# Lightweight convolution and a three-way maxout FFN on one core: weights loaded in two column pieces, an undivided band, block 1's conv copied by ScalarE, x6's load released by a memset

## The chip, the core and the metric

The kernel runs on one core of a Trainium2 chip. The metric is the device time of the whole program in microseconds (us). TensorE (PE) multiplies matrices, and its weight loads are listed apart as PEld; VectorE is DVE, ScalarE is ACT, GpSimd is POOL. SyncE (SP) does no arithmetic here: it issues nearly all the DMAs, from one queue and in program order. Matmul results go to PSUM, from where ScalarE and VectorE copy them on; all other tiles lie in SBUF.

## The reference, cut to what matters

```python
# x: (8, 4160, 192); weight: (8 heads, 7 taps); w1, w2, w3: (192, 768); w_out: (768, 192)
w = softmax(weight, axis=-1)                    # per head
x_pad = 6 zero rows ahead of each sequence
y[b, s, h, :] = sum_k w[h, k] * x_pad[b, s + k, h, :]      # causal conv, 24 channels a head
y = y.reshape(33280, 192)
h = maximum(maximum(y @ w1, y @ w2), y @ w3)
out = h @ w_out                                  # float32, (33280, 192)
```

Every token is convolved over its own and the six tokens before it, with one set of seven weights for each head. Then come three projections to 768 columns, their elementwise maximum, and one projection back.

## The kernel before, in words

**Tiling.** The 33280 tokens are cut into 65 blocks of 512. The 768 hidden columns are cut into 6 groups of 128, called columns 0 to 5 here. The maximum is taken as w3's product plus max(relu(y(w1-w3)), y(w2-w3)). So the kernel builds `wd`, the differences w1-w3 (n=0) and w2-w3 (n=1) for the first 128 input channels and a third slice (n=2) that holds both differences for the last 64 channels (`make_wd`, L318). The share of w3 itself goes through a product of w3 and w_out (`transpose_w3`, `make_m`). For each column `top` (L503) does a relu on ScalarE (L508), which reads the PSUM tile `lp` or `lw`, and a maximum on VectorE (L509), which reads `lq` or `lw` and writes `h`. Then `h` is multiplied by `wo` (L585 and L616).

**The band.** The conv is a matmul against a banded matrix `band`, [128 rows, 8 heads, 134 columns]. Its windows of 38 columns are equal in each quarter of 32 rows. 38 small matmuls (L291) make one window in two PSUM tiles, columns 0 to 27 and 28 to 37. ScalarE copies the first tile and VectorE the second (L299) into all four quarters, heads 5 to 7 first and then heads 0 to 4; block 0's conv begins with the part that needs only heads 5 to 7.

**Dense blocks.** Blocks 0 to 3 are convolved by `conv_dense` (L384). x is loaded into `xin` (float32) and cast to two float16 tiles `xz` by `cast_dense` (L207), where the slots of 32 channels can be given. Two halves of matmuls (n=0: channel slots 0 to 3, n=1: slots 4 and 5) go to two PSUM tiles; `order` says which half is first, and `copies[n]` copies half n to `yd`. The first columns of blocks 0 and 1 are multiplied by `l1_dense`, as full products ("F", from half 0 of `yd`) and half-height products ("H", from half 1 and the slice n=2 of `wd`). Blocks 0 and 1 take turns, two columns at a time.

**Later blocks** (4 and on) are loaded with a layout of 39 rows (`load_x`), their gap rows zeroed first (`zero_x`), cast by GpSimd (`cast_x`, L199), convolved (L375), copied (L415), transposed by a DMA (L429) and multiplied (L521). Their buffers are shared; blocks 4, 5 and 6 have buffers of their own, block 7 takes block 0's. Blocks 5 and 6 are convolved together.

**The order of the work** is written out by hand: each engine runs its instructions as they stand in the program, and semaphores make them wait. SP's DMAs use eight completion semaphores in turn, so a DMA is not issued before the eighth one ahead of it (counting ScalarE's one load) has landed.

**The weights' loads** go to a float32 tile `wall` with the parts `ws` and `w3s`. `load_wa(f)` (L227) loads columns f of the first 128 channels of w3, w1 and w2 in three transfers; `load_wb(f)` (L231) loads the last 64 channels of w1 and w2 in two; L244 loads the last 64 channels of w3 whole. Before, columns 0 to 255, 256 to 511 and 512 to 767 of `load_wa` are three pieces, with `load_wb` of the rest between the second and the third: L243 to L245 and L303 to L305. `copy_w3` (L322, profile line L324) doubles w3's last 64 channels to the other half of the partitions, which the slice n=2 of `wd` needs.

**The start from L695 on** is the part that the diff rearranges. ScalarE and VectorE share the copies of block 1's conv (L702). Then stand ScalarE's second `copy_w3`, GpSimd's subtractions for columns 2 to 5 (L704 to L707), GpSimd's casts of w3 and w_out, and the first products and relus. `zero_x(6)` (L715, profile line L140) is ScalarE's zeroing of block 6's gap rows, and L716 issues the loads of blocks 4, 5 and 6. Block 2's conv stands at L733, block 7's load at L741.

Of the kernel before, what the change touches and what calls it, by code (L numbers as in the profile page):

```python
# [15 lines left out]
P = 128  # L16
KW = 7
PAD = KW - 1
NHEAD = 8
# [5 lines left out]
WIN = 32 + PAD  # L25
# [3 lines left out]
def kernel(  # L29
# [12 lines left out]
    nc = tc.nc  # L42
# [3 lines left out]
    H, KWs = weight.shape  # L46
    assert H == NHEAD and KWs == KW and D == GRP * NHEAD
    DFF = moe_w1.shape[1]
# [9 lines left out]
    for b in range(B):  # L58
        s = nfull * NBLK
        while s < SEQ:  # L60
            n = min(SEQ - s, NBLK - off)
# [24 lines left out]
    NDENSE = 4  # L86
    chunks_of = [conv_chunks(blk) for blk in blocks[:NDENSE]]
    NQ = len(chunks_of[0])
    TOK = 32
# [29 lines left out]
    xin, xbuf, XBUF, loaded = {}, [], 7, set()  # L119

    def get_x(t):

        if not 0 <= t < NB or t in xin:
            return
        if t < XBUF:
            xbuf.append(const.tile([P, NR, D], FP32, name=f"xf_{t}"))
        xf = xbuf[t % XBUF if t < NDENSE + XBUF else NDENSE + (t - NDENSE - XBUF) % 3]
        assert all(v[0] is not xf for v in xin.values())
        xin[t] = [xf, 0, ()]

    def zero_x(t, q0=0, q1=NR, eng=None):
# [4 lines left out]
        if eng is not None:  # L136
# [4 lines left out]
                       in_=bass.AP(tensor=zero.tensor, offset=zero.offset,  # L141
                                   ap=[list(zero.ap[0]), [0, q1 - q0], [1, D]]))

    def load_x(t, eng=nc.sync):
        if not 0 <= t < NB:
            return
        loaded.add(t)
        get_x(t)
        xf = xin[t][0]
        if t < NDENSE:  # L150
            todo = [(0, c[3], c[1] * SEQ + c[2], i) for i, c in enumerate(chunks_of[t])]
        else:
            todo = [(HALF * (i // NR) + (0 if s else LAP), KR if s else TOK,
                     b * SEQ + s - (LAP if s else 0), i % NR) for i, (b, s) in enumerate(rows_of(t))]
        parts = []
        i, n = 0, len(todo)
        row = [c[2] for c in todo]
        while i < n:
            k = i
            while k + 1 < n and todo[k + 1][:2] == todo[i][:2] and row[k + 1] - row[k] == row[i + 1] - row[i]:  # L160
                k += 1
            step = row[i + 1] - row[i] if k > i else 0
            p0, rlen, _, q0 = todo[i]
            q1 = todo[k][3] + 1
            src = bass.AP(tensor=x.tensor, offset=row[i] * D,
                          ap=[[D, rlen], [step * D, q1 - q0], [1, D]])
            eng.dma_start(out=xf[p0:p0 + rlen, q0:q1, :], in_=src)  # L167
            if parts and parts[-1][0] == rlen:
                parts[-1] = (rlen, parts[-1][1], q1)
            else:  # L170
                parts.append((rlen, q0, q1))
            i = k + 1
        xin[t] = [xf, todo[0][0], parts]
# [12 lines left out]
    def cast_x(t):  # L186
        if not 0 <= t < NB:
            return
        xf, p0, _ = xin.pop(t)
        t0, u, nu = place(t)  # L190
        if u == 0:
            pool = x16q if nu >= 4 else x16p
            x16 = pool.tile([P, NHEAD * 4 * 2 * GRP * (5 if nu >= 4 else nu)], FP16, tag="x16", name=f"x16_{t0}")
            x16s[t0] = x16[:, 0:NHEAD * 4 * 2 * GRP * nu].rearrange("p (h j u r c) -> p h j u r c", h=NHEAD, j=4, u=nu, r=2)
        if p0:
            nc.gpsimd.memset(xf[0:p0, 0, :], 0.0)
        K = HALF + KR
        for r in range(2):
            nc.gpsimd.tensor_copy(out=x16s[t0][0:K, :, :, u, r, :].rearrange("p h j c -> p j h c"),  # L199
                                  in_=xf[0:K, 4 * r:4 * r + 4, :].rearrange("p j (h c) -> p j h c", c=GRP))  # L200

    NC, NSLOT, CYC = D // HALF, D // 32, 96
# [1 line left out]
    xz = {t: [const.tile([P, NQ, D], FP16, name=f"xz_{t}_{v}") for v in range(2)] for t in range(2)}  # L204
    xz[2], xz[3] = xz[0], xz[1]

    def cast_dense(t, copies, slots_=range(CYC // 32), keep=False):  # L207
        xf, _, parts = xin[t] if keep else xin.pop(t)
        for v, copy in enumerate(copies):
            if copy is None:  # L210
                continue
            for s in slots_:
                cut = GRP * (32 * s // GRP + 1)
                a, b = (32 * s, cut) if v == 0 else (cut, 32 * s + 32)
                for (rl, q0, q1) in parts:
                    copy(  # L216
                        out=xz[t][v][0:rl, q0:q1, :].rearrange("p q (k c) -> p q k c", c=CYC)[:, :, :, a:b],
                        in_=xf[0:rl, q0:q1, :].rearrange("p q (k c) -> p q k c", c=CYC)[:, :, :, a:b])
# [6 lines left out]
    PW = 2 * P  # L225

    def load_wa(f):  # L227
        for st, n, wsrc in ((w3s, 0, moe_w3), (ws, 0, moe_w1), (ws, 1, moe_w2)):
            nc.sync.dma_start(out=st[:, n, f], in_=wsrc[0:P, f])  # L229
# [51 lines left out]
    nc.vector.reciprocal(out=wrec[:], in_=wrec[:])  # L281
    zero_x(4)
    nc.vector.tensor_scalar_mul(out=line[0:NHEAD, 31:31 + KW], in0=wexp[:, 0:KW], scalar1=wrec[:])
    cast_dense(0, (nc.vector.tensor_copy, nc.gpsimd.tensor_copy), (1, 2), keep=True)
    CUT = 28
    bands_ = []
    for lo, hi, copy in ((0, CUT, nc.scalar.copy), (CUT, WIN, nc.vector.tensor_copy)):
# [5 lines left out]
                             rhs=ident16[:, 0:4 * NHEAD], start=True, stop=True)  # L293
        bands_.append((lo, hi, copy, bps))
    keep_warm((NBLK, NBLK, P), psp, "p")
    for h0, h1 in ((5, NHEAD), (0, 5)):
        for lo, hi, copy, bps in bands_:
            for a in range(4):
                copy(out=band[32 * a:32 * a + 32, h0:h1, 32 * a + lo:32 * a + hi],  # L299
                     in_=bps[:, 0:hi - lo, h0:h1].rearrange("p c h -> p h c"))  # L300
        if h0:
            cast_dense(0, (nc.vector.tensor_copy, nc.gpsimd.tensor_copy), (0,))
    load_wa(slice(PW, 2 * PW))  # L303
    load_wb(slice(PW, DFF))
    load_wa(slice(2 * PW, DFF))  # L305
    nc.sync.dma_start(out=wos[:], in_=moe_w_out.rearrange("(j p) c -> p j c", p=P))
    load_x(2)
    load_x(3)

# [8 lines left out]
    def make_wd(n, j0, j1, eng=nc.vector):  # L318
        f = slice(P * j0, P * j1)
        eng.tensor_sub(out=wd[:, n, f], in0=ws[:, n, f], in1=w3s[:, n // 2, f])  # L320
# [63 lines left out]
    def conv_dense(t, copies, pools=((None, None),) * 2, order=(0, 1)):  # L384


        yd = dense[t] = ydp.tile([P, NC, NBLK], FP16, tag="yd", name=f"yd_{t}")
        for n in order:
            slots_ = ((0, 1, 2, 3), (4, 5, 4, 5))[n]
            pool, tag = pools[n]  # L390
            ps = (pool or psw).tile([P, NBLK], FP32, tag=tag or "w", name=f"D{n}_{t}")
            for (q, b, row_lo, rlen, lo, hi, cc) in chunks_of[t]:
                for v in range(2):
                    for g, s in enumerate(slots_):
                        h = (32 * s + 31 * v) // GRP
                        nc.tensor.matmul(  # L396
                            ps[32 * g:32 * g + 32, lo:hi],
                            lhsT=xz[t][v][0:rlen, q, 32 * s:32 * s + 32],
                            rhs=band[0:rlen, h, cc:cc + hi - lo],
                            start=(v == 0), stop=(v == 1), tile_position=(0, 32 * g))  # L400
            copies[n](out=yd[:, 2 * n, :], in_=ps[:])
# [129 lines left out]
    def l1_dense(tiles, parts="FH"):  # L531

        meet()
        for n, part in enumerate(parts):
            for t, j, pools in tiles:
                for i, (pool, tag) in enumerate(pools):
                    if (t, j, i) not in open_ps:
                        open_ps[t, j, i] = pool.tile([P, NBLK], FP32, tag=tag, name=f"l{tag}{i}_{t}_{j}")
                        begun.discard((t, j, i))
                    if part == "F":  # L540
                        a, b = wd[:, i, P * j:P * (j + 1)], dense[t][:, 0, :]
                    else:
                        a, b = w_of(i, NC - 1, j), y_all(t, i, NC - 1)
                    nc.tensor.matmul(open_ps[t, j, i][:], lhsT=a, rhs=b,  # L544
                                     start=(t, j, i) not in begun, stop=(t, j, i) in begun)
                    begun.add((t, j, i))

    def tops(*tiles):
        for t, j in tiles:
            top(t, j, (open_ps[t, j, 0], open_ps[t, j, 1]))  # L550
# [141 lines left out]
    WPWQ = ((psw, "w"), (psp, "p"), (psw, "w"), (psq, "q"))  # L692
    ACT, DVE = nc.scalar.copy, nc.vector.tensor_copy
    GP = nc.gpsimd.tensor_copy
    conv_dense(0, (ACT, ACT), order=(1, 0))  # L695
    cast_dense(1, (DVE, GP), (1, 2, 0))
    zero_x(5, eng=nc.gpsimd)
    make_wd(0, 0, 2)
    make_wd(1, 0, 2)
    copy_w3(ACT, 0, 2)  # L700
    make_wd(2, 0, 2)
    conv_dense(1, (DVE, ACT), order=(1, 0))  # L702
    copy_w3(ACT, 2, 6)
    for n in range(NC):  # L704
        make_wd(n, 2, 4, nc.gpsimd)
    for n in range(NC):
        make_wd(n, 4, 6, nc.gpsimd)  # L707
    cast_w3(0, 6)
    GP(out=wo[:], in_=wos[:])
    l1_dense([(0, 0, PQ), (0, 1, PQ)], "F")  # L710
    l1_dense([(0, 0, PQ), (0, 1, PQ)], "H")
    tops((0, 0), (0, 1))
    l1_dense([(1, 0, WW), (1, 1, WW)], "HF")
    tops((1, 0), (1, 1))
    zero_x(6)  # L715
    for t in range(NDENSE, XBUF):  # L716
        load_x(t)
    l1_dense([(0, 2, PQ), (0, 3, PQ)], "FH")
    tops((0, 2), (0, 3))
# [11 lines left out]
    first_hidden(0)  # L731
    first_hidden(1)
    conv_dense(2, (ACT, DVE), (WW[0], PQ[1]))  # L733
    cast_x(4)
    cross(2, ACT, DVE)
    make_m(0)
# [114 lines left out]
```

## Time and profile before

| what | us |
|---|---|
| median of 3 runs | 453.19 (453.03 to 454.11) |
| the profiled execution | 454.16 |
| its span | 452.4 |
| PE busy in the span | 445.5 |
| VectorE, ScalarE, GpSimd busy | 354.6, 320.2, 207.6 |
| first product of layer 1 on PE begins | 8.94 |
| mean granted TensorE clock | 1.00 |

The profile lists each engine's instructions with start and length, what each engine waited for, the DMA queues with their packets, and a "chain": the work that ended last, followed back from the last instruction, each step to what released it. A time with two decimals is one from the span's start. The DMA share is the mean busy share of the 16 DMA engines. Queue q1 holds SP's transfers, q8 and q14 carry instructions.

### The profile page before, as it was taken

To read this page: it belongs to the slowest core of one execution; us is meant where nothing else is said; L and a number is where in the kernel's file an instruction comes from. 1 tells how busy PE (TensorE), PEld (TensorE's weight loads), DVE (VectorE), ACT (ScalarE), POOL (GpSimd) and SP (SyncE) were. 2 spreads that over 40 slices of the span, in tenths; PEclk is the share of its full clock that TensorE was granted. 3 is DMA by queue.
4 is the path that set the end of the run, shared out by engine and by line. 5 is a ranking of instruction groups with operands and counts; after the bars stand their busy time and mean duration, and the time that the engine had idled before them with its cause. 6 is when DMAs were issued, how large, how long until landed. Compare 5 with 4: busy or idle time off the path is not lost.

```text
span 452.4 us, 18264 instructions
## 1 busy us (share of the span) xinstructions
PE 445.5 (98%) x7576; PEld 409.8 (91%) x7576; DVE 354.6 (78%) x607; ACT 320.2 (71%) x601; POOL 207.6 (46%) x239
## 2 busy tenths in 40 slices
PE   7999999999999999999999999999999999999997
PEld 4469999999999989999999999999999999999996
DVE  6668787878878787787887787887887887887775
ACT  6967767767777677676676776777776776776664
POOL 5864836556463533724824635525533644224000
PEclk9999999999999999999999999999999999999999
DMA  7968987696885659649649748657649668152123
GB/s 197 239 181 167 203 186 197 155 217 171 170 220 147 165 137 205 162 121 199 167 127 198 178 110 191 191 114 193 178 112 197 172 157 143 54 136 75 58 71 106
DMA packets 128163, 72.01 MB, mean 159 GB/s; under 512 B 52305, under 2 KB 127888, under 8 KB 128080
## 3 DMA queue, kind: packets, MB, share of 16 engines
q1 hardware_dynamic: 127919, 70.75, 65.9%
q8 instruction: 59, 0.97, 0.9%
q14 instruction: 25, 0.20, 0.2%
q10 hardware_dynamic: 160, 0.10, 0.1%
HBM read 33.28 MB, written 25.56 MB: 130 GB/s over the span
## 4 chain that ended last, share of the span: by engine, by line
PE 96%; DMA 1%; ACT 1%; SPq 1%; issue 1%; DVE 0%; ACTq 0%
PE po L585 36%; PE lq L521 32%; PE lp L521 22%; PE G L375 3%; DMA wall<-in_moe_w_dram 1%; ACT r L508 1%; PE D L396 1%; PE po L643 0%; PE po L616 0%; PE lw L544 0%; SPq L229 0%; SPq L167 0%; PE pm L355 0%; ACT wall L324 0%; PE lq L544 0%
## 5 line engine op out<-in xcount | busy, mean ns | idle before, releaser
L585 PE MATMUL po<-wo,h 64*128 64x192 f16 x3024 | 331.7, 243 | 0.0
L509 DVE TENSOR_TENSOR h<-r,lq 128x512 f16<-128x512 f16 x384 | 263.0, 686 | 86.2 <-ACT r L508 76.3
L508 ACT ACTIVATE r<-lp 128x512 f16<-128x512 f32 x384 | 228.9, 597 | 113.8 <-PE lp L521 103.0
L521 PE MATMUL lp<-yp,wd 64*128 64x512 f16 x1098 | 295.6, 376 | 0.0
L521 PE MATMUL lq<-yp,wd 64*128 64x512 f16 x1098 | 295.5, 376 | 0.0
L585 PEld LDWEIGHTS <-h 64*128 64x128 f16 x3024 | 242.7, 94 | 5.4 <-issue 4.1
L521 PEld LDWEIGHTS <-wd 64*128 64x128 f16 x2268 | 181.7, 94 | 14.8 <-issue 0.2
L199 POOL CAST x<-xf 103x768 f16<-103x768 f32 x122 | 97.3, 825 | 114.4 <-DMA xf<-in_x_dram 99.6
L585 PE MATMUL po<-m,yp 64*128 64x192 f16 x720 | 140.3, 243 | 0.0
L438 POOL COPY yp<-yp 64x1536 f16<-64x1536 f16 (+1 forms) x70 | 90.9, 1298 | 86.0 <-DMA yp<-ys 49.1
L593 DVE TENSOR_TENSOR o<-a,po 128x384 f32<-128x384 f32 x126 | 69.0, 547 | 0.0
L585 PEld LDWEIGHTS <-yp 64*128 64x128 f16 x720 | 66.3, 94 | 0.1
L592 ACT COPY a<-po 128x384 f32<-128x384 f32 x126 | 59.6, 473 | 0.0
L415 ACT CAST ys<-G 128x480 f16<-128x480 f32 (+1 forms) x53 | 25.4, 530 | 9.5 <-PE G L375 9.2
L415 DVE CAST ys<-G 128x480 f16<-128x480 f32 (+1 forms) x53 | 30.1, 610 | 0.0
L375 PE MATMUL G<-x,band 39*32 39x240 f16 (+3 forms) x1024 | 16.5, 242 | 0.0
L375 PEld LDWEIGHTS <-band 39*32 39x32 f16 x1024 | 10.2, 92 | 4.6 <-issue 4.1
L521 PE MATMUL lq<-yd,wd 64*128 64x512 f16 x36 | 9.7, 376 | 0.0
L521 PE MATMUL lp<-yd,wd 64*128 64x512 f16 x36 | 9.7, 376 | 0.0
L544 PEld LDWEIGHTS <-wd 128*128 128x128 f16 (+1 forms) x48 | 3.0, 95 | 7.3 <-issue 1.7
L396 PEld LDWEIGHTS <-xz 112*32 112x32 f16 x320 | 4.1, 96 | 2.9 <-issue 1.4
L216 POOL CAST xz<-xf 112x160 f16<-112x160 f32 (+2 forms) x18 | 5.1, 328 | 3.2 <-DMA xf<-in_x_dram 3.0
(75 smaller groups left out, 100.0 us busy)
## 6 DMA issues: line engine op xcount, KB each, us to landing
xf<-in_x_dram SPq DMA_DIRECT2D x113, 234.0 KB
out_dram<-o SPq DMA_DIRECT2D x62, 384.0 KB
xf<-in_x_dram SPq DMA_DIRECT2D x7, 204.8 KB
wall<-in_moe_w_dram SPq DMA_DIRECT2D x11, 128.0 KB
xf<-in_x_dram SPq DMA_DIRECT2D x3, 420.0 KB
yp<-ys SPq DMA_TRANSPOSE x70
out_dram<-o SPq DMA_DIRECT2D x5, 192.0 KB
wos<-in_moe_w_out_dram SPq DMA_DIRECT2D x1, 576.0 KB
```

What stands on the lines that cost most here:

```text
L199: nc.gpsimd.tensor_copy(out=x16s[t0][0:K, :, :, u, r, :].rearrange("p h j c -> p j h c"), in_=xf[0:K, 4 * r:4 * r + 4, :].rearrange("p j ( ...
L216: copy(out=xz[t][v][0:rl, q0:q1, :].rearrange("p q (k c) -> p q k c", c=CYC)[:, :, :, a:b], in_=xf[0:rl, q0:q1, :].rearrange("p q (k c) -> ...
L375: nc.tensor.matmul(G[2 * (k // per) + i][TOK * j:TOK * (j + 1), k % per, :], lhsT=band[row, h, HALF * i + LAP:HALF * i + KR], rhs=x16s[t0] ...
L396: nc.tensor.matmul(ps[32 * g:32 * g + 32, lo:hi], lhsT=xz[t][v][0:rlen, q, 32 * s:32 * s + 32], rhs=band[0:rlen, h, cc:cc + hi - lo], star ...
L415: copy(out=slots[t][:, i % 2, :, :, GRP * h0:GRP * (h0 + per)].rearrange("p u r (h c) -> p h (u r) c", c=GRP), in_=G[i][:].rearrange("p h ...
L438: nc.gpsimd.tensor_copy(out=yp[HALF * i:HALF * (i + 1), 1, :, :, :, :].rearrange("p i u k n -> p (i u k n)"), in_=yp[HALF * (1 - i):HALF * ...
L508: nc.scalar.activation(out=r[:], in_=ps[0][:], func=AF.Relu)
L509: nc.vector.tensor_max(out=hs[t][:, j, :], in0=r[:], in1=ps[1][:])
L521: nc.tensor.matmul(ps[i][:], lhsT=w_of(i, c, j), rhs=y_all(t, i, c), start=(n == 0), stop=(n == NC - 1))
L585: nc.tensor.matmul(ps[b0, i][:, s % 2, :], lhsT=a, rhs=b, start=first, stop=last)
L592: nc.scalar.copy(out=a[:], in_=ps[s - 1, 0][:])
L593: nc.vector.tensor_add(out=outs[t][:, s - 1:s + 1, :], in0=a[:], in1=ps[s - 1, 1][:])
```

## The change

1. `load_wa` is called twice, with columns 0 to 255 and 256 to 767, and `load_wb` follows the second: 11 transfers for w1 to w3, not 14 (with the three for x0 and x1: 14, not 17).
2. `cast_dense(0)` is done whole ahead of the band's copies. Each engine copies its band tile for all 8 heads at once into three quarters, and GpSimd copies the fourth from the first (SBUF to SBUF). Block 0's conv takes the halves in the order 0, 1.
3. Both halves of block 1's conv are copied by ScalarE. The second `copy_w3` stands behind the first two relus, and the subtractions are written between the products; their order on GpSimd stays n=0, 1, 2 for columns 2 and 3, then for columns 4 and 5.
4. Block 6's load is issued behind block 2's conv. `release_x` first has VectorE write one zero into the buffer of block 6; as VectorE does this after its copy of block 2's conv, and the load must wait for it, the load can't be issued earlier.

PE's instructions and their order are otherwise the same.

```diff
+    def release_x(t):
+
+        get_x(t)
+        nc.vector.memset(xin[t][0][TOK:TOK + 1, 0, 0:1], 0.0)
+        load_x(t)
...
-    cast_dense(0, (nc.vector.tensor_copy, nc.gpsimd.tensor_copy), (1, 2), keep=True)
+    cast_dense(0, (nc.vector.tensor_copy, nc.gpsimd.tensor_copy))
...
-    for h0, h1 in ((5, NHEAD), (0, 5)):
-        for lo, hi, copy, bps in bands_:
-            for a in range(4):
-                copy(out=band[32 * a:32 * a + 32, h0:h1, 32 * a + lo:32 * a + hi],
-                     in_=bps[:, 0:hi - lo, h0:h1].rearrange("p c h -> p h c"))
-        if h0:
-            cast_dense(0, (nc.vector.tensor_copy, nc.gpsimd.tensor_copy), (0,))
-    load_wa(slice(PW, 2 * PW))
+    for lo, hi, copy, bps in bands_:
+        for a in range(3):
+            copy(out=band[32 * a:32 * a + 32, :, 32 * a + lo:32 * a + hi],
+                 in_=bps[:, 0:hi - lo, :].rearrange("p c h -> p h c"))
+    nc.gpsimd.tensor_copy(out=band[96:P, :, 96:96 + WIN], in_=band[0:32, :, 0:WIN])
+    load_wa(slice(PW, DFF))
     load_wb(slice(PW, DFF))
-    load_wa(slice(2 * PW, DFF))
     nc.sync.dma_start(out=wos[:], in_=moe_w_out.rearrange("(j p) c -> p j c", p=P))
...
-    conv_dense(0, (ACT, ACT), order=(1, 0))
+    conv_dense(0, (ACT, ACT))
...
-    conv_dense(1, (DVE, ACT), order=(1, 0))
+    conv_dense(1, (ACT, ACT), order=(1, 0))
+    make_wd(0, 2, 4, nc.gpsimd)
+    make_wd(1, 2, 4, nc.gpsimd)
+    l1_dense([(0, 0, PQ), (0, 1, PQ)], "F")
+    l1_dense([(0, 0, PQ), (0, 1, PQ)], "H")
+    tops((0, 0), (0, 1))
     copy_w3(ACT, 2, 6)
-    for n in range(NC):
-        make_wd(n, 2, 4, nc.gpsimd)
+    make_wd(2, 2, 4, nc.gpsimd)
     for n in range(NC):
         make_wd(n, 4, 6, nc.gpsimd)
     cast_w3(0, 6)
     GP(out=wo[:], in_=wos[:])
-    l1_dense([(0, 0, PQ), (0, 1, PQ)], "F")
-    l1_dense([(0, 0, PQ), (0, 1, PQ)], "H")
-    tops((0, 0), (0, 1))
     l1_dense([(1, 0, WW), (1, 1, WW)], "HF")
     tops((1, 0), (1, 1))
     zero_x(6)
-    for t in range(NDENSE, XBUF):
+    for t in range(NDENSE, XBUF - 1):
         load_x(t)
...
     conv_dense(2, (ACT, DVE), (WW[0], PQ[1]))
+    release_x(6)
     cast_x(4)
```

## The prediction, made before the changed kernel ran

> **What bounds the kernel now.** I read the page first: TensorE is busy almost throughout.
>
> ```profile
> PE 445.5 (98%) x7576; PEld 409.8 (91%) x7576; DVE 354.6 (78%) x607; ACT 320.2 (71%) x601; POOL 207.6 (46%) x239
> ```
>
> The waits of PE from 30 us on list nothing, so no edit can gain there: the matmuls are the same, and every edit of the diff lies in the first 30 us. The time changes only by how much earlier or later PE reaches its unbroken stretch. So next came the chain of work that ended last, in its first 45 us (start, length, what):
>
> ```profile
> 3.71 6.13 DMA wall<-in_moe_w_dram
> 9.86 0.40 ACT wall L324
> ...
> 15.12 0.61 ACT r L508
> 15.75 0.70 DVE h L509
> 16.49 0.38 PE lq L544
> ...
> 26.99 0.89 PE D L396 x61
> 27.88 0.84 issue
> ```
>
> Three things are to be seen. The start hangs on one transfer, the rest of w3 (L244), issued at 3.71 and landed at 9.84. From there to 16.49 the chain runs over ScalarE. From 16.49 PE runs almost without a break, except for 0.84 us at 27.88, called "issue": a wait for nothing that the profile shows. Then ScalarE's own timeline:
>
> ```profile
> 9.86 0.40 ACT L324 COPY wall<-wall 64x256 f32<-64x256 f32 x1 [1.79 <-DMA wall<-in_moe_w_dram]
> 10.29 0.58 ACT L401 CAST yd<-D 128x512 f16<-128x512 f32 x1
> 10.90 0.62 ACT L324 COPY wall<-wall 64x512 f32<-64x512 f32 x1
> 11.54 1.08 ACT L508 ACTIVATE r<-lp 128x512 f16<-128x512 f32 x2
> 12.51 1.09 ACT L508 ACTIVATE r<-lw 128x512 f16<-128x512 f32 x2
> 13.63 1.47 ACT L140 CAST xf<-idle 32x1536 f32<-32x1536 f16 x1
> 15.12 1.09 ACT L508 ACTIVATE r<-lp 128x512 f16<-128x512 f32 x2
> ```
>
> There is no gap over 0.03 us between 9.86 and 15.12. The third pair of relus (L508 at 15.12: block 0's columns 2 and 3) stands behind the zeroing of x6 (L140), and VectorE's max behind it frees the PSUM buffer that `lq` of column 4 takes at 16.49. What is added to ScalarE ahead of 15.12 therefore arrives at PE.
>
> **The band and the head: 0.** ScalarE now makes 3 copies of 8x28=224 elements instead of 4 of 84 (217 ns) and 4 of 140 (264 ns). By that slope, 0.84 ns an element, one takes 0.335 us (an estimate), and three from 4.71 end at 5.74, not 6.73. VectorE makes 3 of 80 elements; from 178 ns at 30 and 198 ns at 50 that is 0.23 each, done near 5.8 behind the three casts of x0. GpSimd's copy of the last quarter (32x304) has no row; the nearest are a 112x80 cast (0.26) and a 64x1536 copy (1.30). I take 0.4, near the 112x240 cast (0.39). Block 0's conv then runs from about 5.85, at the worst 6.7, to 6.95 or 7.8; before it ended near 7.3. Nothing follows from it either way: block 1's conv waits for x1's casts (VectorE and GpSimd, 7.15 to 8.15) and takes 0.9 us, and the first l1 matmul at 8.94 waits for `wd`, which VectorE subtracts from 8.25 on, when the weights land.
>
> **Block 1's copy on ScalarE: +0.55.** VectorE's L401 at 10.92 (0.68) goes, but VectorE was then idle 0.56 us until ScalarE's relu came, so nothing is gained. ScalarE gets the copy, 0.585 us. L324's second part only changes places with the first two relus. The first relu cannot start before PE's half product of column 0 (11.06 + 0.39, near 11.5); before it started at 11.54, so 0.05 to 0.1 of the copy is cover. The third pair of relus begins at 15.12 + 0.5 to 0.6 = about 15.67, `lq` of column 4 at about 17.05, and all behind it moves along. Bounds +0.5 and +0.6.
>
> **Weights in two pieces: 0, bounds 0 and +1.0.** What is issued ahead of L244 is unchanged, so I leave its landing at 9.84. Behind it each of three transfers now carries 256 KB. In order of issue, counted in KB from the start, w2's second piece ended at 1928 before and ends at 2312 now; the second half-height pair (L233) at 2184 before and 2568 now. Before, that pair let GpSimd go on at 12.66, and the transfer which then ended at 2568 (w2's third piece) at 15.47:
>
> ```profile
> 12.66 0.73 POOL L320 TENSOR_TENSOR wd<-wall 128x256 f16<-128x256 f32 x1 [0.33 <-ACT r L508]
> ...
> 15.47 1.42 POOL L320 TENSOR_TENSOR wd<-wall 128x256 f16<-128x256 f32 x2 [1.03 <-DMA wall<-in_moe_w_dram]
> ```
>
> (The relu named in the first row is no input of that subtraction; the inputs are the pair and L324.) So the pair now lands between 12.66 and 15.47. The queue was nearly empty from 9.4 to 10.2 (DMA share 0.24 to 0.41 in fifths of a us), and this room is now used; at the 308 KB/us between the landings at 1544 (10.55) and 2184 KB, 384 KB more is 1.25 us: 13.9. I take that. The subtraction then ends at 14.65, PE's half products of columns 2 and 3 plus block 1's matmuls (0.43 + 1.3) end near 16.4, and column 4 waits for its relu until 16.4 anyhow: nothing is lost. From 13.9 on PE is late by what the landing is late, less what the relu's delay hides; a landing at 15.47 puts the relu at 16.7 instead of 15.67, +1.0. What GpSimd saves later (its wait of 1.03 us goes, the third pieces being there) pays back the same delay: w3's cast starts near 16.8 in both.
>
> SP issues three transfers fewer (0.43 us each). SP is not on the path at that point; it brings wos, x2, x3 and x4 forward by 1 to 1.5 us. GpSimd's casts of x2 start only at 19.56, behind other work: 0.
>
> **x6 released late: -0.84, bounds 0 and -0.99.** Is the "issue" gap one of instructions not there yet? The page gives queue q8 59 packets, 0.97 MB, for 15152 PE instructions: 64 bytes each, so 256 to a packet. Packets moved at 7 to 8, 13 to 14, 26 to 27 and 29 to 30 us. PE stopped behind its 959th listed instruction (with some unlisted ones, 1024 = 4x256). The stretch 26 to 27:
>
> ```profile
> q1 hardware_dynamic: 136, 0.10, 36.7%
> q8 instruction: 1, 0.02, 7.0%
> ```
>
> At one boundary earlier, some 240 listed instructions back, PE stood near 22.8 us; had the packet been asked for there, it waited over 3 us, and the x loads held the DMA share at 0.9 from 19 to 24. After the stop the next packet moved within 1.3 us. So I read the gap as a fetch stuck behind x4 to x6. x6 is 468 KB, 2.1 us at the 220 KB/us of that stretch; without it, and with the queue brought forward, the loads end near 22 to 23 and the packet moves near 24.3. It landed at most 2.7 us after it moved before (26.0 to 28.72), so by 27; PE needs it at 27.88 + 0.55. The stall goes; VectorE's zeroing waits and PSUM leave slack there (ScalarE idles from 28.2 to 30.28). -0.99 is the weight load's idle time at the same spot.
>
> The Trainium skill speaks against this gain: "Runtime: NRT & Kernel Launch", Instruction fetch mechanics, says PE's buffer holds 2048 instructions, is refilled by blocks of 256, and that crossing a block's end is mostly hidden. By that rule the gap would not be a fetch and the sum would be +0.55; the row of 0.84 us decides here.
>
> The release costs: a memset of one element on VectorE (0.06, the 1x1 row of L238) ahead of its half of block 2's crossing copy, which ended at 24.59, while PE needs it at 24.85: covered. SP then waits for it at 24.7; behind it stands x7, which waited for ScalarE's zeroing until 25.46 anyhow, and then the store at 27.33. x7 moves by up to 1 us. x6 is cast at 29.69 and its conv on PE is at 36.95; even with L244's 6.1 us it lands at 30.8, casts end at 32.4: covered by 4.5 us. 0.
>
> **Sum.** 0 + 0.55 + 0 - 0.84 = -0.3 us. The profiled execution took 454.16 (span 452.4 and 1.76 around it); it becomes 453.9. The median of the runs shown is 453.19, 0.97 lower; I carry the difference over: 452.9.
>
> **Rivals.**
> 1. The release doesn't do what it is for (the gap is no fetch, or the fetch waits again behind x5): +0.55, 453.75. For it: the share was only 0.36 at 25 to 26 and the packet still waited. Against it: that tail was of the same loads. 0.15.
> 2. Late weights, the slower side: the half-height pair lands at 15.47, as the same count of KB did before, and PE's half products of columns 2 and 3 wait for `wd`. It decides from 13.9 on. +0.55 + 1.0 - 0.84 = +0.7, 453.9; with rival 1 on top +1.55, 454.75. For it: the 15.47 row. Against: those pieces were then issued 1.5 to 2 us later than this pair. 0.18, of which 0.06 with the stall kept.
> 3. ScalarE's copy is hidden (the zeroing or relus start as before because PE or a landing set them): -0.84, 452.35. For it: only 0.1 us of cover is seen. 0.10.
> 4. The landing at 9.84 itself moves. Each us counts fully: earlier by 1 gives 451.9 with the stall gone; later by 1, because double pieces share the engines with it, gives 453.9. 0.05 earlier, 0.04 later.
>
> The forecast has 0.48. A difference within 0.3% (1.36 us) can't be told from no change here. Over that on the fast side is only part of rival 4 and 3 together: 0.05. On the slow side rival 2 with the stall kept, and parts of 4: 0.10. The rest, 0.85, is within. The range runs from rival 3 with a little of 4 (452.1) to rival 2 (454.2).
>
> **What would show it.** Right: no gap over 0.3 us on PE near 28; a q8 packet near 24; ScalarE's third relu pair at 15.6 to 15.75; `lq` of column 4 near 17.05; x6's issue near 24.7. Wrong: L320's third subtraction on GpSimd after 14.7, a gap called "issue" at another place of PE, L324's first copy away from 9.86, or any wait of PE behind 30 us.

## The result, and the profile after

| | before | after |
|---|---|---|
| median of 8 runs each, us | 453.57 (452.90 to 454.19) | 454.94 (454.32 to 456.48) |
| ratio | | 1.0033, 95% interval [1.0021, 1.0045] |
| the profiled execution, us | 454.16 | 454.36 |
| its span, us | 452.4 | 452.6 |

The change costs 1.37 us by the medians and 1.67 us by the means, against a forecast of -0.3. The time lies outside the range that was given (452.1 to 454.2). All means and ratios below leave out one run, of 1633.43 us, of the kernel with two pieces alone.

The two profiled executions are only 0.2 us apart, and this must be kept in mind in what follows: the one of before is close to the slowest of its eight runs, the one of after is the second fastest of its eight. A single pair of traces can't show where 1.4 us went. It can show waits that came and waits that went, and these were then tested by runs.

The line of busy times on the page of after differs from that of before by 0.3 us at most for PE, VectorE and ScalarE, and by 0.8 us for GpSimd:

```profile
PE 445.7 (98%) x7576; PEld 408.5 (90%) x7576; DVE 354.3 (78%) x602; ACT 320.0 (71%) x597; POOL 208.4 (46%) x240
```

The chain that ended last in after, in its first 45 us (start, length, what), no longer runs over the rest of w3 and ScalarE:

```profile
8.35 5.10 DMA wos<-in_moe_w_out_dram
13.61 0.73 POOL wd L323
14.39 0.39 PE lp L547
...
23.05 0.69 DVE yd L404
23.88 1.44 DVE yd L410
25.36 0.37 PE lq L524
```

The gap of 0.84 us called "issue" is not in it. In its place are a subtraction on GpSimd (the load of w_out in front of it is what the profile infers; w_out is no input of it, and the weights' pieces were moving at the same time) and a copy on VectorE which takes 1.4 us where it took 0.5. ScalarE's timeline in after:

```profile
8.16 0.40 ACT L327 COPY wall<-wall 64x256 f32<-64x256 f32 x1 [0.41 <-DMA wall<-in_moe_w_dram]
8.59 1.07 ACT L404 CAST yd<-D 128x512 f16<-128x512 f32 x2
9.71 1.08 ACT L511 ACTIVATE r<-lp 128x512 f16<-128x512 f32 x2
...
12.57 1.47 ACT L140 CAST xf<-idle 32x1536 f32<-32x1536 f16 x1
14.81 1.08 ACT L511 ACTIVATE r<-lp 128x512 f16<-128x512 f32 x2 [0.77 <-PE lq L547]
```

Its first copy starts 1.70 us earlier than in before: the rest of w3 landed earlier. Yet the third pair of relus, at 14.81, is only 0.31 us earlier, and now waits 0.77 us for PE. PE waits for GpSimd, as the first subtractions for columns 2 and 3 on GpSimd's timeline show, and then PE's own rows:

```profile
11.98 1.41 POOL L323 TENSOR_TENSOR wd<-wall 128x256 f16<-128x256 f32 x2 [2.93 <-DMA wall<-in_moe_w_dram]
...
22.02 3.15 POOL L205 CAST x<-xf 103x768 f16<-103x768 f32 x4
```

```profile
12.76 0.39 PE L547 MATMUL lp<-yd,wd 128*128 128x512 f16 x1 [1.47 <-POOL wd L323]
...
25.36 0.37 PE L524 MATMUL lq<-yd,wd 64*128 64x512 f16 x1 [0.47 <-DVE yd L410]
```

The first subtraction waits for w3 and w1, the two transfers that now carry four columns each (256 KB). In before it began at 10.92. So PE, 1.8 us ahead when it began column 0's half product (9.29 against 11.06), was 0.35 us behind when it began column 4 (16.23 against 15.88). At the very next product PE waited in before (0.23 us, for VectorE's maximum) and not in after, so a fairer end of this stretch is matmul 256, the first behind the products of columns 0 to 5: up to there PE needed 9.86 us in after and 8.41 in before, and 0.32 us of the lead was left (19.15 against 19.47). It was 0.53 us at matmul 479, 0.29 at 607 and nothing at 735. From 37.98 on the matmuls of both traces run in step, to the last.

### The profile page after: what moved, and what is told of

It is laid out like the page before. It is cut to its first block, busy times and chain, and to the rows that moved or that the text cites. A ratio compares the mean times of both kernels' runs of the same rounds, so it can differ in the third digit from the quotient of the medians.

```text
span 452.6 us, 18255 instructions
## 1 busy us (share of the span) xinstructions
PE 445.7 (98%) x7576; PEld 408.5 (90%) x7576; DVE 354.3 (78%) x602; ACT 320.0 (71%) x597; POOL 208.4 (46%) x240
## 4 chain that ended last, share of the span: by engine, by line
PE 96%; SPq 2%; DMA 1%; DVE 1%; issue 0%; POOL 0%; POOLq 0%
PE po L588 36%; PE lq L524 31%; PE lp L524 22%; PE G L378 3%; DMA wos<-in_moe_w_out_dram 1%; PE lw L547 1%; SPq L235 1%; SPq L239 1%; PE D L399 0%; PE po L646 0%; PE po L619 0%; PE lp L547 0%; DVE yd L410 0%; SPq L173 0%; POOL wd L323 0%
## 5 line engine op out<-in xcount | busy, mean ns | idle before, releaser
L378 PE MATMUL G<-x,band 39*32 39x240 f16 (+3 forms) x1024 | 16.5, 242 | 0.0
L222 POOL CAST xz<-xf 112x80 f16<-112x80 f32 (+2 forms) x18 | 5.5, 353 | 1.4 <-DMA xf<-in_x_dram 1.4
L588 PE MATMUL po<-m,yd 64*128 64x192 f16 x36 | 5.9, 244 | 0.0
```

What stands on the lines that cost most here:

```text
L222: copy(out=xz[t][v][0:rl, q0:q1, :].rearrange("p q (k c) -> p q k c", c=CYC)[:, :, :, a:b], in_=xf[0:rl, q0:q1, :].rearrange("p q (k c) -> ...
L378: nc.tensor.matmul(G[2 * (k // per) + i][TOK * j:TOK * (j + 1), k % per, :], lhsT=band[row, h, HALF * i + LAP:HALF * i + KR], rhs=x16s[t0] ...
L588: nc.tensor.matmul(ps[b0, i][:, s % 2, :], lhsT=a, rhs=b, start=first, stop=last)
```

## The experiments

Each kernel was run with the kernel before on the same chip. "Difference" is that of the means, with a 95% interval; the ratio has its own. The starts of the same matmul were compared by its place in PE's list, counted from 0: number 240 is the first product of column 4, and 479, 607 and 735 stand 128 apart. All of PE's gaps called "issue" of over 0.2 us stand at 479 and 607, but for one of 0.34 us at 71.43 in the run with x6's load undone. 128 matmuls with their weight loads are 256 instructions, one packet of queue q8.

**1. How far one trace and one run can be trusted.** The kernel before again:

> The kernel before, unchanged, to see how the start varies from run to run. Theory 1 (late pieces): the two profiles on record are not of the same start; w3's rest landed at 9.84 us before and 8.16 after with the same transfers ahead of it, so before's median of 453.57 should hold runs whose start is as early as after's, and a new profile has L324's first copy anywhere between 8.1 and 9.9, with a span that is lower by up to 1.3 us when it is early. Theory 2 (the change itself makes the landing early): L324's first copy is at 9.8 to 9.9 again. Ratio 1.000 either way.

453.13 us, ratio 1.0009 [0.9989, 1.0029]; its 12 runs lie between 452.3 and 454.67, with one at 457.88. In its profiled execution (454.45) the gap is there again, and a second one: 0.7 and 0.5 us. The kernel after again:

> The changed kernel, unchanged, for a second profile. Ratio 1.0033 again (interval 1.0021 to 1.0045). If the losses are built in and not an accident of one profile: the crossing copy of block 2 on VectorE takes over 1.2 us again, GpSimd's first subtraction for columns 2 and 3 is again more than 1.0 us later than the end of block 1's products on PE, and there is no gap of 0.84 us on PE near 28.

454.78 against 453.60, ratio 1.0023 [1.0006, 1.0041], difference +1.04 +-0.50. The loss is there again, and there is no gap near 28 us. The other two marks of its trace are not: the crossing copy took 0.55 us, and GpSimd's first subtraction began at 12.44, before block 1's products ended on PE (12.64). But this execution (453.96) was the second fastest of its twelve, so it does not settle whether the two cost time in the others. ScalarE's first copy of w3's rest, which I had taken as fixed at 9.86, began at 9.68 and 9.47 in these two; over all 17 profiled executions it lies between 8.16 and 10.00, with the same transfers ahead of it. The two traces on record are near the two ends. As the same kernel after began it at 8.16 and at 9.47, I read the 1.70 us between them as chance, not as the change.

**2. Each part alone, on the kernel before.** The undivided band:

```diff
-    for h0, h1 in ((5, NHEAD), (0, 5)):
...
-            for a in range(4):
...
+        for a in range(3):
...
+    nc.gpsimd.tensor_copy(out=band[96:P, :, 96:96 + WIN], in_=band[0:32, :, 0:WIN])
...
-    conv_dense(0, (ACT, ACT), order=(1, 0))
+    conv_dense(0, (ACT, ACT))
```

> The kernel before with the undivided band, x0's casts whole ahead of it and block 0's conv in the order 0, 1 alone. Every theory, and the prediction: 0, since the first l1 matmul waits for the weights; ratio 0.999 to 1.001. If the head does matter, the matmuls of blocks 0 and 1 move on PE by more than L324's first copy does.

Ratio 0.9999 [0.9987, 1.0012], difference -0.15 +-0.50. No cost can be told from noise. The weights in two pieces:

```diff
-    load_wa(slice(PW, 2 * PW))
+    load_wa(slice(PW, DFF))
     load_wb(slice(PW, DFF))
-    load_wa(slice(2 * PW, DFF))
```

> The kernel before with the weights in two column pieces alone. Theory 1 (late pieces): GpSimd's first subtraction for columns 2 and 3 starts at 11.5 to 12.5 instead of 10.92, PE waits for it, and this part alone costs most of the loss: +0.8 to +1.6 us. Rival (ScalarE's extra copy): 0 for this part. Third (VectorE's crossing copy of block 2 collides with GpSimd's casts because x4 and x5 come early): +0.5, with a crossing copy of 1.4 us instead of 0.50 on VectorE near 24 us.

Ratio 1.0015 [1.0004, 1.0027], difference +0.56 +-0.47. GpSimd's first subtraction for columns 2 and 3 in this kernel:

```profile
12.71 1.41 POOL L319 TENSOR_TENSOR wd<-wall 128x256 f16<-128x256 f32 x2 [3.40 <-DMA wall<-in_moe_w_dram]
```

From column 0's half product to matmul 256 PE needed 9.41 us here and 8.41 in before, though ScalarE had no more to do. The third theory's mark was there too: the crossing copy took 1.50 us and PE waited 0.43 us for it, so the +0.56 is not shown to be the late pieces' alone. Block 1's copies on ScalarE, with the new order of products and subtractions:

```diff
-    conv_dense(1, (DVE, ACT), order=(1, 0))
-    copy_w3(ACT, 2, 6)
+    conv_dense(1, (ACT, ACT), order=(1, 0))
...
     tops((0, 0), (0, 1))
+    copy_w3(ACT, 2, 6)
```

> The kernel before with block 1's conv copied by ScalarE alone (both halves, and the second copy of w3's rest behind the first two relus). Rival (ScalarE's extra copy, as I predicted): +0.5 to +0.6 us, the third pair of relus at 15.6 to 15.75 if the start is at 9.86. Theory 1 (late pieces): 0 to +0.3, since PE or a landing and not ScalarE sets columns 2 to 5 when the start is early.

Ratio 1.0020 [1.0007, 1.0033], difference +0.77 +-0.50. The same stretch of PE took 9.12 us, 0.71 more than in before, and 0.60 more than the mean of 8.52 in the nine traces with three pieces and the shared copy; the forecast was +0.55. ScalarE's rows of this kernel carry it:

```profile
9.78 1.07 ACT L401 CAST yd<-D 128x512 f16<-128x512 f32 x2
11.18 1.09 ACT L508 ACTIVATE r<-lp 128x512 f16<-128x512 f32 x2 [0.33 <-PE lq L544]
...
15.53 0.60 ACT L508 ACTIVATE r<-lp 128x512 f16<-128x512 f32 x1
```

Counted from its first copy, at 9.35, the third pair of relus comes 6.18 us later, in before 5.26; 0.33 of that is a wait for a product. x6's load behind block 2's conv:

```diff
-    for t in range(NDENSE, XBUF):
+    for t in range(NDENSE, XBUF - 1):
         load_x(t)
...
     conv_dense(2, (ACT, DVE), (WW[0], PQ[1]))
+    nc.vector.memset(xin[6][0][TOK:TOK + 1, 0, 0:1], 0.0)
+    load_x(6)
```

> The kernel before with x6's load released behind block 2's conv alone. If the 0.84 us gap on PE is an instruction fetch behind the x loads: gap gone, and 0 to -0.9 us; what the after profile shows too, gaps at the next two boundaries (256 instructions on, 0.25 and 0.29 us there), gives part of it back, so -0.3 is the likeliest. If the gap is no fetch: it stays at the same instruction and the time is the same.

Ratio 1.0014 [1.0003, 1.0025], difference +0.78 +-0.30, where -0.84 was forecast. Its trace does what was expected of it: the gap at 479 is gone. The loss is not to be seen in it: from matmul 240 to 735 PE took 21.31 us, and 21.17 to 22.57 in the six traces that leave x6 where it was (before twice, band, two pieces, block 1's copy, and x6's load undone, below). But VectorE's crossing copy is long:

```profile
24.40 0.06 DVE L734 MEMSET xf<- 1x1 f32 x1
24.49 1.33 DVE L407 COPY yd<-yd 64x512 f16<-64x512 f16 x1
```

**3. Each part undone, in the kernel after.** The first two of these and the kernel after itself (+1.04) shared a chip. Three column pieces as before:

```diff
-    load_wa(slice(PW, DFF))
+    load_wa(slice(PW, 2 * PW))
     load_wb(slice(PW, DFF))
+    load_wa(slice(2 * PW, DFF))
```

> The changed kernel with the weights in three column pieces as before. Theory 1 (late pieces): this part alone cost 0.8 us in its own run, so the ratio falls from 1.0033 to about 1.0015, and GpSimd's first subtraction for columns 2 and 3 is no later than 0.5 us behind PE's need. Collision theory (VectorE's crossing copy held by GpSimd's casts): the release alone brought the collision too, so it stays, with a copy of over 1.2 us, and the ratio stays above 1.0015.

Ratio 1.0001 [0.9985, 1.0017], difference +0.12 +-0.59; against the kernel after itself -0.91 +-0.65. GpSimd's first subtraction started at 11.34, but PE's stretch to matmul 256 took 9.13 us, against 9.86 and 9.12 in the two traces of after: against the second of them the gain is not to be seen there. x6 loaded where it was:

```diff
-    for t in range(NDENSE, XBUF - 1):
+    for t in range(NDENSE, XBUF):
         load_x(t)
...
-    release_x(6)
```

> The changed kernel with x6's load where it was. Release theory (held back x6 lets x5 land early, GpSimd's four casts run in one piece and hold VectorE's crossing copy; it also moves the fetch's waits to later boundaries): ratio falls by 0.0010 to 0.0020, to about 1.0018, with a crossing copy of 0.5 us. Rival: two pieces alone also brought the collision, so it stays at 1.3 to 1.5 us and the ratio stays at 1.0033.

Ratio 1.0008 [0.9995, 1.0021], difference +0.33 +-0.44; against the kernel after -0.71 +-0.51. Here too the release costs. And its trace has no gap at 479 although x6 is not released: that gap is not in every execution with x6 in its old place. Block 1's conv copied by both engines as before:

```diff
-    conv_dense(1, (ACT, ACT), order=(1, 0))
+    conv_dense(1, (DVE, ACT), order=(1, 0))
+    copy_w3(ACT, 2, 6)
```

> The changed kernel with block 1's conv copied by VectorE and ScalarE and the second copy of w3's rest back in its place. ScalarE theory: this part alone cost 0.77 us (+-0.50), 0.55 by its length; so the ratio falls by 0.0012, to about 1.0015. Late pieces: in the changed kernel PE waits for the second piece and not for ScalarE, so the ratio stays at 1.0023 to 1.0033.

Ratio 1.0025 [1.0015, 1.0036], difference +1.04 +-0.39: as large as the kernel after. Its stretch to matmul 256 took 9.46 us, as with two pieces alone (9.41). With both parts in, it took 9.12 us in three traces (after again, x6 undone, the cast that waits, below), as with ScalarE's copy alone, and 9.86 in after. So the late piece and ScalarE's copy do not add up: one hides behind the other, and which of them sets the stretch differs between executions.

**4. Is it the collision of VectorE's copy with GpSimd's casts?** In after, x4 and x5 land earlier, so GpSimd's four casts run back to back (22.02 to 25.17, shown above) where before had a pause of 0.34 us. VectorE's crossing copy of block 2 runs beside them:

```profile
23.79 0.06 DVE L147 MEMSET xf<- 1x1 f32 x1
23.88 1.43 DVE L410 COPY yd<-yd 64x512 f16<-64x512 f16 x1
```

It ends at 25.31, 0.14 us behind the last cast; in before it took 0.50, and PE had no wait for it. Unbroken casts alone do not make it long, as after again shows:

```profile
22.53 3.21 POOL L205 CAST x<-xf 103x768 f16<-103x768 f32 x4
24.50 0.55 DVE L410 COPY yd<-yd 64x512 f16<-64x512 f16 x1
```

In 13 of the 16 traces in which VectorE makes this copy it ended 0.14 to 0.15 us behind the end of a cast: in nine behind the cast beside which it had begun, in four (the long ones) behind the next. In the other three it took 0.29 us. What decides between one cast and two is not shown. To take the collision away, GpSimd reads one element of the copy's result before it casts x5:

```diff
     load_x(7)
+    nc.gpsimd.tensor_copy(out=mark[HALF:HALF + 1, 0:1], in_=dense[2][HALF:HALF + 1, 1, 0:1])
     cast_x(5)
```

> The changed kernel with one element copied by GpSimd ahead of x5's casts, from the half that VectorE's crossing copy writes, so that x5's casts wait for that copy. Collision theory: the copy takes 0.5 us again, PE's wait of 0.5 us for it near 25 us goes, and the ratio falls by 0.0010 to about 1.0020; x5's casts have over 4 us of slack. Rival (late pieces alone): the copy is short, but the time stays, because something else is as late.

The copy took 0.29 us and PE's wait for it went, but the ratio is still 1.0021 [1.0007, 1.0036], difference +0.81 +-0.56. PE came to 607 earlier and waited there, the weight load's row in this kernel:

```profile
32.95 0.11 PEld L589 LDWEIGHTS <-h 64*128 64x128 f16 x4 [1.05 <-issue]
```

The same wait added to the release alone:

> The kernel before with x6's late release, and x5's casts on GpSimd waiting for VectorE's crossing copy. The release alone cost 0.78 us (+-0.30). Collision theory: that was the crossing copy held for 1.33 us by the casts, so with the wait the copy takes 0.3 to 0.6 us and the time is that of before or 0.3 us less. Fetch theory (x6's load now runs at 25 to 28 us, ahead of the block of PE instructions that the boundary near 32.5 us needs): PE gets there earlier, waits there instead, and +0.3 to +0.8 remains, with a gap called issue of 0.3 to 0.9 us at the 607th matmul.

Ratio 1.0006 [0.9995, 1.0018], difference +0.31 +-0.45: between no loss and the release's +0.78, and both lie within its interval or at its edge. The copy took 0.80 us here, beside x4's casts, so the wait took the collision only in part away; PE had a gap of 0.21 us at 607. So I tried the other way, both halves of the crossing copy on ScalarE, with the release:

```diff
-    cross(2, ACT, DVE)
+    cross(2, ACT, ACT)
```

> The kernel before with x6's load released by VectorE's memset, and both halves of block 2's crossing copy on ScalarE. Theory (VectorE's crossing copy is held by GpSimd's casts, and this is most of the release's +0.78 us): no copy over 0.7 us, ScalarE has some 0.5 us more to do there: +0.1 to +0.5 us. Rival (the cost is that of x6's packets ahead of the later fetches): +0.7 to +1.2 us.

Ratio 1.0016 [1.0006, 1.0027], difference +0.57 +-0.50. No copy was held, and the loss stayed; it lies between the two theories' expectations. But ScalarE's extra work has a price of its own in the trace:

```profile
24.70 0.37 PE L521 MATMUL lp<-yd,wd 64*128 64x512 f16 x1 [0.76 <-ACT m L357]
```

So this run does not separate the theories. The collision is real but not shown to be what the release costs. A gap at 607 was there once more:

```profile
32.83 0.11 PEld L585 LDWEIGHTS <-h 64*128 64x128 f16 x3 [0.54 <-issue]
```

**5. Is "issue" a fetch behind loads?** Four more loads of 234 KB behind x7's, into a weight buffer that is no longer read; nothing uses them:

```diff
     load_x(7)
+    for n in range(4):
+        p0, m = HALF * (n // 2), 2 * (n % 2)
+        nc.sync.dma_start(out=wall[p0:p0 + KR, m:m + 2, :].rearrange("p n (a d) -> p (n a) d", d=D),
+                          in_=bass.AP(tensor=x.tensor, offset=n * SEQ * D, ap=[[D, KR], [TOK * D, 2 * NDENSE], [1, D]]))
```

> The kernel before with four added loads of 234 KB, into a part of the weights' float32 tile that is read no more, issued right behind block 7's load: twice x6's bytes, at the place of the release. Nothing reads them. Fetch theory: the q8 packet that moved at 29.96 moves at 31 us or later, and PE shows a gap called issue of over 0.5 us at its 607th matmul, at 32.5 to 34 us: +0.5 to +2 us. Rival (the gaps called issue are no fetch, or loads do not delay a fetch): no gap there, time within 0.3 us, unless a wait for x7, x8 or a transpose is shown instead.

457.28 us, ratio 1.0090 [1.0068, 1.0112], difference +3.94 +-1.09 (6 runs). The waits of PE from 24 us on (what it waited for: us in total, times, longest):

```profile
PE po L585 <- issue: 2.9, 1, 2.9
PE D L396 <- issue: 1.3, 1, 1.3
```

No engine reads these loads, and PE stops at 607 for some 3 us. The q8 packet that it needs there moved at 34.14, against 29.96 in before. Loads ahead of a packet hold PE up: shown.

**6. What is the stall worth at most, and what does the late load cost?** The kernel before without x6's load at all (block 6's casts read x5's buffer), and the same with GpSimd's wait for the crossing copy:

```diff
-    for t in range(NDENSE, XBUF):
+    for t in range(NDENSE, XBUF - 1):
         load_x(t)
+    loaded.add(6)
+    xin[6] = [xin[5][0], xin[5][1], ()]
```

> The kernel before without x6's load: block 6's casts read x5's buffer instead, so block 6's conv is that of block 5's tokens, and 468 KB less are loaded; x7 is issued where it was. Theory (the release takes the stall of 0.84 us away, but x5 then lands earlier, GpSimd's casts run back to back over VectorE's crossing copy, and x6's own packets later stand ahead of the next fetches): the gap of 0.84 us at PE's 28th us goes, the later fetches have no x6 ahead of them, the crossing copy still takes 1.3 to 1.5 us: -0.5 to 0 us. Rival (the stall is hardly there in most executions, so its removal is worth nothing, and what the release cost lies in the casts): 0 to +0.8 us, like the release's +0.78.

> As the run without x6's load, and GpSimd waits for VectorE's crossing copy before it casts x5. Theory: neither stall nor collision nor a later load ahead of a fetch: -0.5 to -1.0 us, which is the most that the release could ever have gained. Rival: the stall is hardly there in most executions: within 0.3 us of the kernel before.

Ratios 0.9985 [0.9970, 1.0000] and 0.9990 [0.9978, 1.0001], differences -0.57 +-0.46 and -0.57 +-0.45. Neither trace has a wait of PE behind 24 us, and from matmul 240 to 735 PE took 20.55 and 20.50 us, less than in any other trace. So taking x6's load from where it stood does gain, about 0.57 us. GpSimd's wait adds nothing to it, but this says little of the collision: the crossing copy took 0.35 us in the first trace, where 1.3 to 1.5 was expected, and 0.82 in the second. The release on the same chip (with the crossing copy on ScalarE) was +0.57, or 1.13 +-0.54 us more than no load, but that holds the wait for ScalarE shown above. The two kernels with GpSimd's wait differ in the late load alone; they ran on two chips, and their differences against before are 0.88 +-0.64 apart. By both, the late load costs time against none. That it costs more than its removal gained rests on the release alone (+0.78) and on its undoing.

## Why the prediction was wrong, point by point

**The step that failed: "x6 released late: -0.84", with its price of 0 for the load in its new place.** Alone it measured +0.78 +-0.30; undone, it gave back 0.71 +-0.51. Three things were wrong with it.

First, the gain was read from one profiled execution that was slow for its kernel. The same gap is absent in four traces that leave x6 where it was (the band, the two pieces, block 1's copy, the release undone). The runs without x6's load put it at 0.57 +-0.46, which is about the most that any release could have brought.

Second, I asked of the late load only when its own data are needed ("covered by 4.5 us"), and not what it would stand in front of. The reading of the gap as a fetch fits the extra loads, and should have been used again: in all 17 traces the packet for 607 moved only after PE had passed 479, and PE is through that block 4.4 us later where nothing stops it (4.8 for the next). From the start of the packet to PE's going on were 2.5 to 2.9 us wherever PE waited at 479 or 607 for over 0.2 us. So by an estimate a packet may start some 1.5 to 1.9 us (4.44 less 2.5 to 2.9) after PE has passed 479; later than that, each us counts. x6, issued at 23.92 and 24.27 in after, and x7 behind it, fall just into this. From PE's passing of 479 to the packet for 607 it was, with x6 released, 1.73 to 2.65 us, 2.12 in the mean of eight traces (after, after again, three pieces, the cast that waits, the conv shared; the release alone and with either remedy). With x6 in its old place it was 0.69 to 2.57, 1.48 in the mean of six traces (before twice, two pieces, block 1's copy, band, release undone); without x6's load 0.99 and 1.42. In after PE took 0.25 and 0.29 us longer than the undisturbed 4.44 and 4.81 for the two blocks behind 479; the weight loads' rows:

```profile
32.87 0.11 PEld L588 LDWEIGHTS <-h 64*128 64x128 f16 x4 [0.42 <-issue]
...
37.97 0.09 PEld L588 LDWEIGHTS <-h 64*128 64x128 f16 x1 [0.36 <-issue]
```

In this trace the stall was in part handed to the next two fetches. That loads delay fetches is shown by the extra loads; that this is what the release costs is not. The release's own trace has no such gap, and from matmul 240 to 735 the eight traces with x6 released took 21.46 us in the mean, the six with x6 in its old place 21.61: the loss that the runs show by their times is not in these traces, and executions without the profiler can't be looked into. So it is shown that the late load costs time, and not why; fetches and the held copy are the two causes that were seen.

Third, loads brought forward were put at 0, and the crossing copy was "covered" by 0.26 us of slack: the earlier landing let GpSimd's casts close up, and the copy took 1.33 to 1.50 us in four traces (after, two pieces, the release, the conv shared), and PE waited 0.4 to 0.5 us for it. In after again and with x6 undone the casts were as close and the copy took 0.55 and 0.29. The Trainium skill, "Advanced Engine Details and Errata", VectorE Performance Modes, says that VectorE's second port to SBUF is shared with GpSimd, so that GpSimd's instructions and those of VectorE that use both ports block each other. That agrees with the rows (0.29 us with no cast beside it in after with the cast that waits, 1.43 in after, ending 0.14 us behind a cast); I did not weigh it.

**Weights in two pieces: 0 was too low; +0.56 +-0.47 alone and -0.91 +-0.65 when undone, within the bounds 0 and +1.0.** Rival 2 had the side and the place right (PE's products of columns 2 and 3, behind `wd`), but not the transfer. I followed the half-height pair, the last of the second pieces. It was the first two, w3 and w1: each had doubled, so what columns 2 and 3 need from them came only with what columns 4 and 5 need. Counted from ScalarE's first copy of w3's rest, which takes a part of the chance of the start out, GpSimd's first subtraction for columns 2 and 3 began 1.06 to 2.94 us later in the eleven traces with three pieces (mean 1.95) and 1.72 to 3.82 us later in the six with two (mean 2.97). The spreads overlap, so no single pair of traces shows it; the means are 1.0 us apart (0.85 counted from the span's start). That this was the cause of the whole +0.56 is not shown, since two pieces alone brought the held copy too.

**Block 1's copy on ScalarE: +0.55 was right** where the weights are in time: +0.77 +-0.50 by time, +0.60 to +0.71 in the trace. Undone in the kernel after it gave nothing back (+1.04 still): the second piece then set the same stretch of PE. That the three parts alone add up to +2.11, and the whole change to +1.04 and +1.67 in two measurements, fits such shadows.

**The band: 0 was right** (-0.15 +-0.50).

**What was to show it.** Right: no gap near 28, a q8 packet near 24 (23.25). The third pair of relus came at 14.81 and not at 15.6, `lq` of column 4 at about 16.5 and not at 17.05, because the start was 1.70 us earlier and the late pieces took only a part of that back. x6's issue was at 23.92, not 24.7. Two of the named signs of error were there: L324's first copy (now L327) away from 9.86, and gaps called "issue" at other places, on the weight loads at 32.87 and 37.97. The third subtraction, begun at 13.61, was before 14.7, and still the second rival was at work: that sign was set on the wrong transfer.

The sum also carried an offset of 0.97 from the profiled execution to the median. For after that offset has the other sign (454.36 against 454.94).

No version tried that loads all of x beats the kernel before: its time could be told from none of the band alone, three pieces in after, the release with the cast that waits, and x6's load undone in after (0.9999, 1.0001, 1.0006, 1.0008).

## What to carry to other kernels

When a transfer is moved away from a stall, list what it will stand in front of in its new place, instruction fetches among it, and not only when its own data are needed. When transfers are merged, look at the first consumer of each merged piece: it now waits for bytes that only a later one needs. Before a gap of less than a us is booked as a gain, look whether a second profiled execution has it, and where the profiled one stands among the runs.

## What the runs showed of the hardware that was not expected

- **Instruction fetches reached only one block ahead.** PE's large gaps called "issue" stood at matmuls 128 apart, and the packet for 607 moved 0.69 to 4.94 us after PE had passed 479, never before. The Trainium skill, "Runtime: NRT & Kernel Launch", Instruction fetch mechanics, calls such crossings mostly hidden; here PE waited 0.2 to 2.9 us at them beside the loads of the first 38 us; behind 38 us no wait of PE is listed in before or after.
- **A VectorE copy of 64x512 float16 took 0.29 to 1.50 us** by what GpSimd did beside it: 0.29 with no cast running (after with the cast that waits), 0.35 to 0.82 where it ended behind the cast beside which it had begun, 1.33 to 1.50 where it ended behind the next one.
- **The landing of the same early transfers varied by 1.8 us** from one profiled execution to the next (ScalarE's first copy of w3's rest from 8.16 to 10.00), more than the whole change was worth.
